# One visit of TensorE to attention for each chunk from the fifth tile on, in a fused state-space and MoE kernel

## The chip, the cores and the metric

The kernel runs on one core of a Trainium2 chip. The metric is the device time of one execution in microseconds. Five engines work side by side: TensorE (PE, with its weight loads shown apart as PEld), VectorE (DVE), ScalarE (ACT), GpSimd (POOL) and SyncE (SP), which here issues the DMAs.

## The reference

A chunked linear recurrence (called attention here) gives x of 3072 tokens and 256 features; an MLP follows, with g = h - tanh(h).

```python
log_a = np.log(np.clip(a, 1e-06, 1.0))            # batch 4, 8 heads, 768 steps
for c in range(nc):
    cum = np.cumsum(la, axis=-1)
    L = np.exp(cum[:, :, :, None] - cum[:, :, None, :]) * causal
    CB = np.einsum('bhin,bhjn->bhij', Cc, Bc)       # n = 16
    y_intra = np.einsum('bhij,bhjd->bhid', CB * L, xc)   # d = 32
    y_inter = np.einsum('bhin,bhnd->bhid', Cc, state) * np.exp(cum)[..., None]
    y[:, :, sl] = y_intra + y_inter
    state = decay_full[:, :, None, None] * state + np.sum(Bx, axis=2)
x = attn_out.transpose(0, 2, 1, 3).reshape(B * S, H * D)
h = x @ w_in                                        # 256 -> 2048
g = h - np.tanh(h)
return g @ w_out                                    # 2048 -> 256
```

## The kernel before

**The MLP.** The 3072 tokens form 12 tiles of 256; the 2048 hidden features form 8 units of 256. For each tile and unit there is one call of `mm1` (x by w_in into the PSUM tile ph) and one of `mm2` (g by w_out into the PSUM tile o). Every operand is split into a high part and a remainder (xh and xl, wh and wl, gh and gl), and three of the four products are kept, so a call is 12 matmuls of 128x256. A call is a **block** below; there are 192. Between the two, ACT takes the tanh (L542), DVE subtracts (L546), ACT makes gh (L550) and DVE gl (L557). There are two buffers of ph. The first four tiles are swept two units at a time (`SWEEPS`), since the weights arrive and are converted (`conv`, L280 to L304) meanwhile; from the fifth tile on each tile runs through its eight units.

**Attention.** The reference's chunks of 32 are taken in chunks of 112 steps, seven for each batch (the last has 96), 28 in all. The first 16 rows of a chunk's matrix carry the state of the chunk before. A chunk takes two pieces of work on TensorE:

- the **scores piece**, in `chunk_a`: four bf16 matmuls give the differences of the cumulated logs (L435) and eight small ones C B^T (L441), into the PSUM tile att. Behind it come the exponential on ACT (L445), the product on DVE (L449) and the causal select on POOL (L452), which makes lt. There is one buffer of att.
- the **y piece**, in `chunk_y`: eight matmuls give y (L477), and eight with a stationary operand of 16 columns give the next state (L485; left out for a batch's last chunk). It needs lt. Behind it ACT copies the state to the next chunk's x (L490) and makes xh (L497), and DVE makes xl (L502).

Where TensorE leaves the blocks for one or more such pieces and comes back, the text says a **visit**.

**The order** is made at build time. The code above calls `op(engine, cost, fn, r=..., w=...)`; nothing is issued then. `Order.issue` plays a list schedule of all operations with these costs 16 times, with priorities from a backward pass plus a random jitter of a fixed seed, keeps the shortest and issues each engine's instructions in that order. An `op` is never split, so the instructions of one `fn` stay together on their engine. Since priorities and jitter go by an operation's number, another set of operations gives another order everywhere. The main loop at the end lays out the calls of `mm1`, `mm2`, `chunk_a` and `chunk_y`.

```python
op("PE", 0.65, fn_p, r=[d["n_bc"], l_c[s], r_c[s]], w=[n_a])        # L456, scores
op("PE", 0.5 if last else 0.7, fn, r=[*k["n_l"], d["p_x"][cg], d["n_bw"]], w=[n_y])  # L505, y and state
```

Of the kernel before, what the change touches and what calls it, by code (L numbers as in the profile page):

```python
# [29 lines left out]
NCK = NB * CPB  # L30
# [13 lines left out]
NPH, NL, NSW, NRAW, NGB, LAG, WARM = 2, 3, 4, 2, 3, 2, 8  # L44
# [3 lines left out]
class Order:  # L48
# [12 lines left out]
    def slot(self, tag, bufs):  # L61
        k = self.count[tag] = self.count.get(tag, -1) + 1
        self.fresh[f"{tag}#{k}"] = tag, f"{tag}#{k - bufs}"
        return f"{tag}#{k}"
# [126 lines left out]
def tile_ssm_moe(ctx: ExitStack, tc: tile.TileContext, a, x, bn, bc, wts, out):  # L191
# [11 lines left out]
    op = Order()  # L203
    slot = op.slot
    grp = {g: {} for g in range(NG)}
    chs = {c: {} for c in range(NCK)}
    raws, gs, po, n_po, obs, misc = {}, {}, {}, {}, {}, {}

    chunks, ends = {}, 0
# [4 lines left out]
    wv, wm, pts, n_pt = {}, {}, {}, {}  # L214
    seq = {b: {} for b in range(NB)}
    KB = P * 1024

    SPAN = slice(len(chunks[0]), len(chunks[0]) + 7), slice(len(chunks[0]) + 7, NCK)


    def load_bc(G):
# [5 lines left out]
        def fn(i):  # L227
            if i == 0:
                d["bc"] = p2.tile([P, 2, CPG * (P + Q)], F32, tag="bc", name=f"bc{G}", bufs=NGB)
            nc.sync.dma_start(out=d["bc"][32 * i : 32 * i + N], in_=bc[G, i])  # L230

        for i in range(4):
            op("SP", 0.42, lambda i=i: fn(i), w=[d["n_bc"]], dma=KB // 2)
    def load_x(G):

        d = grp[G]
        d["n_x"] = slot("x", NGB)
        d["p_x"] = op.pieces(d["n_x"], CPG)

        def fn():  # L240
            d["x"] = p2.tile([P, CPG, H * D], F32, tag="x", name=f"x{G}", bufs=NGB)
            nc.sync.dma_start(out=d["x"], in_=x[:, G * CPG : (G + 1) * CPG])

        op("SP", 0.42, fn, w=d["p_x"], dma=2 * KB)

    def load_b(G):
# [5 lines left out]

        op("SP", 0.42, fn, w=[d["n_b"]], dma=KB)

    def load_w(u):
        name = raws[u, 0] = op.pieces(slot("raw", NRAW), 2)

        def fn(i):
            if i == 0:
                raws[u] = p2.tile([P, 2, 512, 2], U32, tag="raw", name=f"raw{u}", bufs=NRAW)  # L260
            nc.sync.dma_start(out=raws[u][:, i].rearrange("p k two -> p (k two)"), in_=wts[:, u, i])

        for i in range(2):
            op("SP", 0.42, lambda i=i: fn(i), w=[name[i]], dma=4 * KB)

# [74 lines left out]
    def qlen(ck):  # L340
        return QL if ck % CPB == CPB - 1 else Q
# [13 lines left out]
    def first_tile():  # L355
# [39 lines left out]
        for ck in range(len(chunks[0])):  # L395
# [12 lines left out]
            if ck in (0, 2):  # L408
# [7 lines left out]
                for i in range(4):  # L416
                    for j in range(2):
                        op("SP", 0.42, lambda i=i, j=j, sl=sl: get_parts(i, j, sl), r=["cum3"], w=[(l_c, r_c)[j][s]],
                           dma=(KB // 2, KB)[s])
            chunk_y(ck)  # L420

    def chunk_a(ck):

        d, k, q = grp[ck // CPG], chs[ck], qlen(ck)
        n_l = k["n_l"] = [slot("lt", NL)]
        n_a = k["n_a"] = slot("att", 1)

        def fn_p():  # L430
            at_ = ps_a.tile([P, 4, 4 * P], F32, tag="att", name=f"att{ck}")
            at_ = k["a"] = at_[:, :, 0 : 4 * q].rearrange("p i (k q) -> p i k q", k=4)
            for i in range(4):
                r = slice(32 * i, 32 * i + 9)
                nc.tensor.matmul(out=at_[:, i, 0:2, :], lhsT=lt_c[r, ck], rhs=rt_c[r, :, ck, N : N + q],  # L435
                                 start=True, stop=True)
            bb, cc = operands(ck)
            for w in range(2):
                for i in range(4):
                    r = slice(32 * i, 32 * i + N)  # L440
                    nc.tensor.matmul(out=at_[:, i, 2 + w, :], lhsT=bb[r, w], rhs=cc[r, w, 0:q], start=True, stop=True)  # L441

        def fn_e():
            k["l"] = p3.tile([P, H, Q], F32, tag="lt", name=f"lt{ck}", bufs=NL)
            nc.scalar.activation(k["l"][:, :, 0:q].rearrange("p (i w) q -> p i w q", i=4), k["a"][:, :, 0:2, :], AF.Exp)  # L445

        def fn_m():
            lt = k["l"][:, :, 0:q].rearrange("p (i w) q -> p i w q", i=4)
            nc.vector.tensor_tensor(out=lt, in0=k["a"][:, :, 2:4, :], in1=lt, op=ALU.mult)  # L449

        def fn_s():
            nc.gpsimd.affine_select(out=k["l"][:, :, 0:q], in_=k["l"][:, :, 0:q], pattern=[[0, H], [1, q]],  # L452
                                    compare_op=ALU.is_ge, fill=0.0, base=N, channel_multiplier=-1)

        s = ck >= SPAN[0].stop
        op("PE", 0.65, fn_p, r=[d["n_bc"], l_c[s], r_c[s]], w=[n_a])  # L456
        op("ACT", 0.92, fn_e, r=[n_a], w=n_l)
        op("DVE", 1.08, fn_m, r=[n_a], w=n_l)
        op("POOL", 1.4, fn_s, w=n_l)

    def chunk_y(ck):

        d, k, q = grp[ck // CPG], chs[ck], qlen(ck)
        b, c = divmod(ck, CPB)
        cg = ck % CPG
        n_y = slot("y", 1)
        last = c == CPB - 1
        if c == 0:
            seq[b]["n_xh"] = op.pieces(slot("xh", 2), CPB)
            seq[b]["n_xl"] = op.pieces(slot("xl", 2), CPB)  # L470
        n_xh, n_xl = seq[b]["n_xh"][c], seq[b]["n_xl"][c]

        def fn():
            y = k["y"] = ps_y.tile([P, 2 * H * D], F32, tag="y", name=f"y{ck}")
            for hg in range(2):
                for h in range(4):
                    nc.tensor.matmul(out=y[D * h : D * h + D, hg * Q : hg * Q + q],  # L477
                                     lhsT=d["x"][:, cg, P * hg + D * h : P * hg + D * h + D],
                                     rhs=k["l"][:, 4 * hg + h, 0:q], start=True, stop=True)
            if not last:  # L480

                for w in range(2):
                    for i in range(4):
                        h = 2 * i + w
                        nc.tensor.matmul(out=y[D * i : D * i + N, H * D + D * w : H * D + D * w + D],  # L485
                                         lhsT=d["b"][:, cg, N * h : N * h + N], rhs=d["x"][:, cg, D * h : D * h + D],
                                         start=True, stop=True)

        def fn_c(i):
            nc.scalar.copy(grp[(ck + 1) // CPG]["x"][0:N, (ck + 1) % CPG, 2 * D * i : 2 * D * i + 2 * D],  # L490
                           k["y"][D * i : D * i + N, H * D : H * D + 2 * D])

        def fn_h():
            if c == 0:
                seq[b]["xh"] = p3.tile([P, 2, S], F32R, tag="xh", name=f"xh{b}", bufs=2)
            k["yv"] = k["y"][:, 0 : 2 * Q].rearrange("p (g q) -> p g q", g=2)[:, :, 0:q]
            nc.scalar.copy(seq[b]["xh"][:, :, c * Q : c * Q + q], k["yv"])  # L497

        def fn_l():
            if c == 0:  # L500
                seq[b]["xl"] = p3.tile([P, 2, S], F32R, tag="xl", name=f"xl{b}", bufs=2)
            nc.vector.tensor_tensor(out=seq[b]["xl"][:, :, c * Q : c * Q + q], in0=k["yv"],  # L502
                                    in1=seq[b]["xh"][:, :, c * Q : c * Q + q].bitcast(F32), op=ALU.subtract)

        op("PE", 0.5 if last else 0.7, fn, r=[*k["n_l"], d["p_x"][cg], d["n_bw"]], w=[n_y])  # L505
        if not last:
            for i in range(4):
                op("ACT", 0.2, lambda i=i: fn_c(i), r=[n_y], w=[grp[(ck + 1) // CPG]["p_x"][(ck + 1) % CPG]])
        op("ACT", 0.36, fn_h, r=[n_y], w=[n_xh])
        op("DVE", 0.4, fn_l, r=[n_y, n_xh], w=[n_xl])  # L510
# [92 lines left out]
    def store(t, seg):  # L603
# [20 lines left out]
        for i in range(2):  # L624
            op("SP", 0.42, lambda i=i: fn_d(i), r=[name[i]], dma=KB)

# [17 lines left out]
    rest = p2.tile([P, 2, TT], F32, tag="ob", name="rest")[:, 0].rearrange("p (i q) -> p i q", i=2)  # L644
# [64 lines left out]
    l_c = op.pieces("lt_c", 2)  # L709
    r_c = op.pieces("rt_c", 2)  # L710
# [39 lines left out]
    def get_parts(i, k, sl):  # L750
        src = cum3[i // 2].rearrange("p (e w c) m -> p e w c m", e=2, w=2)[:, i % 2, :, sl].rearrange("p w c m -> p w (c m)")
        if k == 0:
            nc.sync.dma_start(out=lt_c[32 * i + 3 : 32 * i + 9, sl], in_=src)
        else:
            nc.sync.dma_start(out=rt_c[32 * i : 32 * i + 3, :, sl].rearrange("p w c m -> p w (c m)"), in_=src)
# [12 lines left out]
       r=[n_pq2], w=["wdec"])  # L768
# [19 lines left out]
    def plan(g, fn, *args):  # L788
        todo.setdefault(max(g, 0), []).append((fn, args))
# [5 lines left out]
    at_ = {}  # L795
# [2 lines left out]
        for i, ck in enumerate(chunks[t]):  # L798
            at_[ck] = g0 + i * n // len(chunks[t]), min(g0 + i * n // len(chunks[t]) + 1, g0 + n - 1)
    for ck in at_:  # L800
        plan(at_[ck][0], chunk_a, ck)
        plan(at_[ck][1], chunk_y, ck)
        if (ck + 1) % CPG == 0 and ck // CPG + NGB < NG:
            plan(at_[ck][1], group, ck // CPG + NGB)
# [58 lines left out]
```

## Time and profile before

| | us |
|---|---|
| time, median of 3 runs | 346.46 (345.67 to 348.44) |
| the profiled execution's own time | 350.21 |
| span of its trace, first to last instruction | 348.5 |
| PE busy | 333.0 (96%) |
| DVE busy | 228.1 (65%) |
| ACT busy | 193.0 (55%) |
| POOL busy | 53.8 (15%) |

The busy share of an engine is a mean over the whole span; which engine sets the time in a stretch has to be read from that stretch. The profiled execution is one of its own, and lies above the three timed ones.

### The profile page before, as it was taken

The page shows a single profiled execution, that of the slowest core. Times are in us where ns is not written, and L with a number is a line of the kernel's source. Part 1 is how long each engine was busy: PE and PEld are TensorE (multiplying, and loading weights), DVE is VectorE, ACT ScalarE, POOL GpSimd, SP SyncE. Part 2 cuts the span into 40 slices and gives each one's busy share as a digit, 9 for nine tenths or more (in the row PEclk, how much of TensorE's full clock was granted, in tenths as well). Part 3 has the DMA queues.
Part 4 walks back from the last instruction along what each step waited for, and adds up shares of the span by engine and source line. Part 5 has one row for each costly group of instructions (what it writes and reads, how often), then busy time and mean ns, then how long its engine had stood idle before and what let it go on. Part 6 is the DMA issues. An engine that isn't in the chain of part 4 may idle for free.

```text
span 348.5 us, 8864 instructions
## 1 busy us (share of the span) xinstructions
PE 333.0 (96%) x3756; PEld 320.0 (92%) x3756; DVE 228.1 (65%) x339; ACT 193.0 (55%) x403; POOL 53.8 (15%) x69
## 2 busy tenths in 40 slices
PE   9768779999999999999999999999999999999995
PEld 7657678899999999999999999999999999999995
DVE  5799976998998856545645654655645554655552
ACT  8767656986554443544555545544655545543441
POOL 1543343220000100020121210210211110110000
PEclk9868668999999999999999999999999999999999
DMA  6948583570100001111110300300300100000000
GB/s 186 259 115 286 137 282 78 158 184 5 40 3 0 2 32 37 57 30 45 57 46 8 85 2 2 88 2 2 90 3 1 32 2 2 32 0 2 30 2 31
DMA packets 12471, 21.39 MB, mean 61 GB/s; under 512 B 2848, under 2 KB 7648, under 8 KB 12432
## 3 DMA queue, kind: packets, MB, share of 16 engines
q1 hardware_dynamic: 12432, 20.84, 20.7%
q8 instruction: 29, 0.48, 0.6%
q14 instruction: 10, 0.08, 0.1%
HBM read 17.51 MB, written 3.32 MB: 60 GB/s over the span
## 4 chain that ended last, share of the span: by engine, by line
PE 84%; DVE 7%; ACT 2%; issue 2%; DMA 2%; SPq 1%; POOL 0%; DVEq 0%; POOLq 0%; ACTq 0%
PE o L578 38%; PE ph L528 37%; PE y L477 3%; PE att L441 3%; DMA bc<-bc_d 2%; DVE lt L449 1%; PE att L435 1%; DVE wl L304 1%; DVE gl L557 1%; SPq L230 1%; PE y L485 1%; DVE xl L502 1%; DVE wm L293 1%; DVE wm L285 1%; ACT lt L445 1%
## 5 line engine op out<-in xcount | busy, mean ns | idle before, releaser
L542 ACT ACTIVATE g<-ph 128x512 f32<-128x512 f32 x96 | 57.4, 598 | 96.6 <-PE ph L528 95.1
L546 DVE TENSOR_TENSOR g<-ph,g 128x512 f32<-128x512 f32 x96 | 66.1, 690 | 68.2 <-ACT g L542 68.1
L528 PE MATMUL ph<-xh,wh 128*128 128x256 f32 x384 | 101.5, 286 | 0.0
L528 PE MATMUL ph<-xh,wl 128*128 128x256 f32 x384 | 100.1, 283 | 0.4 <-DVE wl L304 0.4
L557 DVE TENSOR_TENSOR gl<-g,gh 128x512 fp32r<-128x512 f32 x96 | 67.3, 701 | 25.8 <-ACT gh L550 24.0
L528 PE MATMUL ph<-xl,wh 128*128 128x256 f32 x384 | 77.1, 282 | 0.0
L528 PEld LDWEIGHTS ph<-xh,wh 128*128 128x128 f32 x384 | 74.0, 193 | 1.0 <-issue 0.4
L528 PEld LDWEIGHTS ph<-xh,wl 128*128 128x128 f32 x384 | 73.8, 192 | 0.7 <-DVE wl L304 0.7
L550 ACT CAST gh<-g 128x512 fp32r<-128x512 f32 x96 | 59.1, 617 | 26.8 <-DVE g L546 25.2
L578 PE MATMUL o<-gh,wh 128*128 128x256 f32 x384 | 64.2, 289 | 0.1
L452 POOL TENSOR_SCALAR_AFFINE_SELECT lt<-lt 128x896 f32<-128x896 f32 (+1 forms) x25 | 30.9, 1236 | 215.6 <-DVE lt L449 214.6
L578 PE MATMUL o<-gl,wh 128*128 128x256 f32 x384 | 60.6, 280 | 0.0
L578 PE MATMUL o<-gh,wl 128*128 128x256 f32 x384 | 60.5, 279 | 0.0
L528 PEld LDWEIGHTS ph<-xl,wh 128*128 128x128 f32 x384 | 59.7, 192 | 0.0
L578 PEld LDWEIGHTS o<-gh,wh 128*128 128x128 f32 x384 | 51.6, 189 | 3.2 <-ACT pt L599 0.3
L578 PEld LDWEIGHTS o<-gl,wh 128*128 128x128 f32 x384 | 51.9, 189 | 0.0
L578 PEld LDWEIGHTS o<-gh,wl 128*128 128x128 f32 x384 | 51.9, 189 | 0.0
L449 DVE TENSOR_TENSOR lt<-att,lt 128x896 f32<-128x896 f32 (+1 forms) x25 | 26.7, 1067 | 5.8 <-ACT lt L445 5.8
L445 ACT ACTIVATE lt<-att 128x896 f32<-128x896 f32 (+1 forms) x25 | 22.5, 901 | 4.9 <-PE att L441 3.5
L490 ACT COPY x<-y 16x64 f32<-16x64 f32 x96 | 19.5, 203 | 7.0 <-DVE xl L502 6.0
L477 PE MATMUL y<-lt,x 128*32 128x112 f32 (+1 forms) x448 | 17.9, 282 | 3.6 <-POOL lt L392 3.3
L477 PEld LDWEIGHTS y<-lt,x 128*32 128x32 f32 x448 | 10.6, 116 | 7.6 <-POOL lt L392 3.6
(70 smaller groups left out, 232.7 us busy)
## 6 DMA issues: line engine op xcount, KB each, us to landing
raw<-w_d SPq DMA_DIRECT2D x16, 512.0 KB
x<-x_d SPq DMA_DIRECT2D x14, 256.0 KB
bc<-bc_d SPq DMA_DIRECT2D x56, 60.0 KB
out_d<-ob SPq DMA_DIRECT2D x24, 128.0 KB
braw<-bn_d SPq DMA_DIRECT2D x14, 112.0 KB
cum<-parts SPq DMA_DIRECT2D x1, 168.0 KB
lt_c<-cum SPq DMA_DIRECT2D x4, 27.0 KB
rt_c<-cum SPq DMA_DIRECT2D x4, 27.0 KB
```

Of the source, the lines that this page charges most:

```text
L441: nc.tensor.matmul(out=at_[:, i, 2 + w, :], lhsT=bb[r, w], rhs=cc[r, w, 0:q], start=True, stop=True)
L445: nc.scalar.activation(k["l"][:, :, 0:q].rearrange("p (i w) q -> p i w q", i=4), k["a"][:, :, 0:2, :], AF.Exp)
L449: nc.vector.tensor_tensor(out=lt, in0=k["a"][:, :, 2:4, :], in1=lt, op=ALU.mult)
L452: nc.gpsimd.affine_select(out=k["l"][:, :, 0:q], in_=k["l"][:, :, 0:q], pattern=[[0, H], [1, q]], compare_op=ALU.is_ge, fill=0.0, base=N, ...
L477: nc.tensor.matmul(out=y[D * h : D * h + D, hg * Q : hg * Q + q], lhsT=d["x"][:, cg, P * hg + D * h : P * hg + D * h + D], rhs=k["l"][:, 4 ...
L490: nc.scalar.copy(grp[(ck + 1) // CPG]["x"][0:N, (ck + 1) % CPG, 2 * D * i : 2 * D * i + 2 * D], k["y"][D * i : D * i + N, H * D : H * D + ...
L528: nc.tensor.matmul(out=ph[:, j, :], lhsT=w_[:, u, 0, k, j * P : (j + 1) * P], rhs=d[("xh", "xl")[p]][:, k, ts], start=p == 0 and k == 0 an ...
L542: nc.scalar.activation(g, gs[t, u][0], AF.Tanh)
L546: nc.vector.tensor_tensor(out=g, in0=ph, in1=g, op=ALU.subtract)
L550: nc.scalar.copy(gh, gs[t, u][1])
L557: on.tensor_tensor(out=gl, in0=g, in1=gh.bitcast(F32), op=ALU.subtract)
L578: nc.tensor.matmul(out=po[t, seg][:, e, :], lhsT=w_[:, u, 1, j, e * P : (e + 1) * P], rhs=g[:, j, :], start=u == seg[0] and k == 0 and j = ...
```

## The change

`chunk_a` no longer registers its operations itself from the fifth tile's first chunk on (`JOINT`, chunk 10). It hands its PE function on, and `chunk_y` of the chunk before registers one PE operation that issues y, the state, and then the next chunk's scores; the operations that follow the scores are registered right after it (`chunk_b`). Up to chunk 9 the scores are an operation of their own, as before. The last chunk's y has no scores behind it. No instruction is added or removed on any engine.

```diff
+    JOINT = chunks[NSW][0]
...
         s = ck >= SPAN[0].stop
-        op("PE", 0.65, fn_p, r=[d["n_bc"], l_c[s], r_c[s]], w=[n_a])
+        k["rest"] = fn_e, fn_m, fn_s
+        k["pe_a"] = fn_p, [d["n_bc"], l_c[s], r_c[s]], [n_a]
+        if ck < JOINT:
+            op("PE", 0.65, fn_p, r=k["pe_a"][1], w=k["pe_a"][2])
+            chunk_b(ck)
+
+    def chunk_b(ck):
+        k = chs[ck]
+        n_l, n_a = k["n_l"], k["n_a"]
+        fn_e, fn_m, fn_s = k["rest"]
         op("ACT", 0.92, fn_e, r=[n_a], w=n_l)
         op("DVE", 1.08, fn_m, r=[n_a], w=n_l)
         op("POOL", 1.4, fn_s, w=n_l)
...
-        op("PE", 0.5 if last else 0.7, fn, r=[*k["n_l"], d["p_x"][cg], d["n_bw"]], w=[n_y])
+        r, w, cost = [*k["n_l"], d["p_x"][cg], d["n_bw"]], [n_y], 0.5 if last else 0.7
+        if JOINT <= ck + 1 < NCK:
+
+            chunk_a(ck + 1)
+            fn_p, r_a, w_a = chs[ck + 1]["pe_a"]
+            op("PE", cost + 0.45, lambda: (fn(), fn_p()), r=r + r_a, w=w + w_a)
+            chunk_b(ck + 1)
+        else:
+            op("PE", cost, fn, r=r, w=w)
...
     for ck in at_:
-        plan(at_[ck][0], chunk_a, ck)
+        if ck < JOINT:
+            plan(at_[ck][0], chunk_a, ck)
         plan(at_[ck][1], chunk_y, ck)
```

TensorE in the fourth batch, before: y and state of chunk 23 and, one `mm2` block later, the scores of chunk 24 (y, att, o: the PSUM tiles; bc: B and C; bw: weighted B; the numbers behind a name count tiles).

```order
L477 MATMUL y_3719<-lt_3665,x_2796 32x112 x8
L485 MATMUL y_3719<-x_2796,bw_2793 16x32 x8
L578 MATMUL o_0_3511<-gh_5_3668,wh 128x256 x4
L578 MATMUL o_0_3511<-gh_5_3668,wl 128x256 x4
L578 MATMUL o_0_3511<-gl_5_3684,wh 128x256 x4
L435 LDWEIGHTS lt_c
L435 MATMUL att_3758<-rt_c,lt_c 128x224
...
L441 MATMUL att_3758<-bc_3069 128x112 x8
L578 MATMUL o_0_3511<-gh_6_3715,wh 128x256 x4
```

TensorE at the same two pieces in the changed kernel (lines moved by 2 to 19).

```order
L488 MATMUL y_3687<-lt_3582,x_2775 32x112 x8
L496 MATMUL y_3687<-x_2775,bw_2777 16x32 x8
L437 LDWEIGHTS lt_c
L437 MATMUL att_3704<-rt_c,lt_c 128x224
...
L443 MATMUL att_3704<-bc_2888 128x112 x8
L597 MATMUL o_0_3569<-gh_4_3651,wh 128x256 x4
```

The block between the two pieces is gone from there; the visit now begins with y and ends with the scores. From y of chunk 9 on, 34 visits have become 19: before, three of the 34 held both pieces, now 18 of the 19 do. Between those 19 the changed order has 18, 30, 6, 4, 12, 4, 7, 5, 4, 12, 4, 12, 4, 7, 5, 4, 12 and 4 blocks, and 10 blocks stand ahead of y of chunk 9, where it was 11.

ScalarE at the same place, before: around the exponential of chunk 24.

```order
L497 CAST xh_3524<-y_3719 128x2x112
L490 COPY x_3165<-y_3719 16x64 x3
L550 CAST gh_7_3756<-g_7_3736 128x512
L490 COPY x_3165<-y_3719 16x64
L445 ACTIVATE lt_3786<-att_3758 128x896
```

ScalarE there in the changed kernel.

```order
L561 ACTIVATE g_6_3717<-ph_6_3670 128x512
L508 CAST xh_3471<-y_3687 128x2x112
L447 ACTIVATE lt_3733<-att_3704 128x896
L569 CAST gh_6_3749<-g_6_3717 128x512
L501 COPY x_3127<-y_3687 16x64 x4
```

The exponential has moved ahead of the state's four copies and of a cast; one cast of y stands between it and the visit.

VectorE in the start-up, before: up to the xl of chunk 9 (y_934), with which the fourth tile's x is complete.

```order
L285 TENSOR_SCALAR wm_845<-raw_702 128x1024
L290 TENSOR_SCALAR wv_837<-wv_837 128x1024
L449 TENSOR_TENSOR lt_843<-att_807,lt_843 128x896
L502 TENSOR_TENSOR xl_804<-y_849,xh_796 128x2x112
L557 TENSOR_TENSOR gl_0_906<-g_0_821,gh_0_879 128x512
L546 TENSOR_TENSOR g_1_891<-ph_1_824,g_1_891 128x512
L293 SCALAR_TENSOR_TENSOR wm_845<-wv_837,wm_845 128x1024
L557 TENSOR_TENSOR gl_1_952<-g_1_891,gh_1_928 128x512
L449 TENSOR_TENSOR lt_911<-att_893,lt_911 128x896
L502 TENSOR_TENSOR xl_804<-y_934,xh_796 128x2x112
```

VectorE there in the changed kernel (chunk 9 is y_884), and what follows it.

```order
L513 TENSOR_TENSOR xl_802<-y_824,xh_779 128x2x112
L299 SCALAR_TENSOR_TENSOR wv_631<-wv_631,wm_655 128x1024
L576 TENSOR_TENSOR gl_0_916<-g_0_804,gh_0_878 128x512
L565 TENSOR_TENSOR g_1_882<-ph_1_845,g_1_882 128x512
L287 TENSOR_SCALAR wm_939<-raw_699 128x1024
L513 TENSOR_TENSOR xl_802<-y_884,xh_779 128x2x112
L292 TENSOR_SCALAR wv_842<-wv_842 128x1024
L576 TENSOR_TENSOR gl_1_964<-g_1_882,gh_1_942 128x512
L306 TENSOR_TENSOR wl<-wv_631,wh 128x1024
L295 SCALAR_TENSOR_TENSOR wm_939<-wv_842,wm_939 128x1024
```

Counted from the kernel's start, one L290, one L293, one L557 and one L449 that stood ahead of this xl now stand behind it; all else ahead of it is the same in kind and number.

## Rows read from the trace of the kernel before

**Rows 1.** Windows: busy us and instructions of each engine, granted TensorE clock, DMA.

```profile
core 0: us, PE busy (x) PEld busy (x) DVE busy (x) ACT busy (x) POOL busy (x), PEclk, DMA share, GB/s
23.40:69.00 45.60, 40.52 (x561) 36.59 (x556) 40.30 (x50) 31.60 (x69) 16.45 (x17) 0.80 0.66 192
50.00:55.00 5.00, 5.00 (x53) 4.67 (x50) 2.88 (x4) 1.76 (x5) 3.35 (x4) 0.50 0.23 41
69.00:314.50 245.50, 245.25 (x2717) 238.54 (x2716) 155.85 (x227) 130.62 (x265) 28.10 (x31) 1.00 0.11 32
86.00:141.50 55.50, 55.50 (x492) 55.50 (x491) 43.17 (x63) 27.32 (x49) 1.77 (x2) 1.00 0.07 22
```

**Rows 2.** Chain of waits, 300 to 312 us: start, length, what; two visits.

```profile
300.40 1.41 PE ph L528 x12
301.81 0.52 PE y L477 x16
...
302.44 1.56 PE o L578 x12
304.00 1.36 PE ph L528 x12
...
308.08 0.19 PE att L435 x4
...
308.73 1.61 PE o L578 x12
310.34 1.41 PE ph L528 x12
```

**Rows 3.** Chain of waits, 248 to 253 us: a visit with both pieces.

```profile
248.88 0.52 PE y L477 x16
...
250.17 1.61 PE o L578 x12
251.78 1.41 PE ph L528 x12
```

**Rows 4.** Chain of waits, 137 to 147 us: a visit of y and state.

```profile
137.66 2.72 PE ph L528 x24
...
142.38 1.61 PE o L578 x12
143.99 2.83 PE ph L528 x24
```

**Rows 5.** Timeline of all engines, 250 to 256 us, behind the visit of rows 3.

```profile
250.03 0.34 ACT L497 CAST xh<-y 128x224 fp32r<-128x224 f32 x1
250.10 0.74 PE L578 MATMUL o<-gh,wh 128*128 128x256 f32 x4
250.31 0.92 ACT L445 ACTIVATE lt<-att 128x896 f32<-128x896 f32 x1
251.26 1.09 DVE L449 TENSOR_TENSOR lt<-att,lt 128x896 f32<-128x896 f32 x1 [0.46 <-ACT lt L445]
252.42 1.37 POOL L452 TENSOR_SCALAR_AFFINE_SELECT lt<-lt 128x896 f32<-128x896 f32 x1 [2.13 <-DVE lt L449]
255.95 0.59 PE L477 MATMUL y<-lt,x 128*32 128x112 f32 x16
```

**Rows 6.** Groups of instructions, shapes apart: busy us and mean ns, idle before.

```profile
L557 DVE TENSOR_TENSOR gl<-g,gh 128x512 fp32r<-128x512 f32 x96 | 67.3, 701 | 25.8 <-ACT gh L550 24.0
L449 DVE TENSOR_TENSOR lt<-att,lt 128x896 f32<-128x896 f32 x21 | 22.8, 1088 | 5.2 <-ACT lt L445 5.2
L293 DVE SCALAR_TENSOR_TENSOR wm<-wv,wm 128x1024 uint32<-128x1024 uint32 x7 | 9.1, 1301 | 0.1
L290 DVE TENSOR_SCALAR wv<-wv 128x1024 f32<-128x1024 f32 x7 | 5.2, 741 | 0.0
```

**Rows 7.** Chain of waits, 50 to 57 us: two blocks of the start-up.

```profile
50.05 2.86 PE o L578 x12
...
54.02 2.25 PE ph L528 x12
```

## The prediction

> **What bounds the kernel now.** I read the windows first, to cut the span into stretches by who waits. From 23.4 to 69 us DVE is busy 40.30 of 45.60 us and PE 40.52, at a mean granted clock of 0.80: weights are converted, the first ten chunks run, and no engine alone sets the time [rows 1]. From 69 to 314.5 us PE is busy 245.25 of 245.50 us at clock 1.00, DVE 155.85 and ACT 130.62 [rows 1]. So in 70% of the span the time is the sum of PE's own work: blocks and visits. The reader should see there that nothing can be gained or lost except in the length of a block, in what a visit costs, or in a wait that does not exist yet.
>
> Then I read the chain of waits for those lengths, and two things show.
>
> First, a visit costs more than its own matmuls. The visit of y and state starts at 301.81 and the next block at 302.44, 0.63 us; but that block takes 1.56 where the one behind it takes 1.36, so 0.20 goes on coming back: 0.83 in all. The scores alone: 308.08 to 308.73, 0.65, and 1.61 against 1.41, together 0.85 [rows 2]. A visit with both: 248.88 to 250.17, 1.29, and again 1.61 against 1.41, together 1.49 [rows 3].
>
> Second, a block has two lengths at the same granted clock of 1.00. It takes 1.41 us ahead of the state visit at 301.81 and 1.36 behind it; behind the scores visit at 308.08 it is 1.41 again [rows 2]. A length holds until the next visit: from 85.7 to 141.7 us, 41 blocks without a visit all run at 1.36 [rows 1, 4]. I sorted all visits from 69 us on by what they end with. Those that end with the scores (16 alone, 3 behind a y piece) are followed by the long block every time, 19 of 19. Those that end with the state's matmuls, whose stationary operand has 16 columns, are followed by the short block 9 times in 12, as at 302.44, and 3 times by the long one, as at 142.38 [rows 2, 4]. The three y pieces without a state do not shorten it. I do not know why; the prediction uses only that it is so.
>
> **The change part by part.**
>
> *Joining.* From y of chunk 9 on there are 34 visits now and 19 in the changed order, so 15 fewer. Each joining saves 0.83 + 0.85 - 1.49 = 0.19 us [rows 2, 3]: what PE pays to leave the blocks and come back, once in place of twice. 15 x 0.19 = 2.9 us saved, all of it on PE, which bounds.
>
> *What a visit ends with.* Every joined visit ends with the scores. So behind chunk 9 no visit is left that ends with the state's matmuls, and by the 19 of 19 every block from there on has the long form. Short blocks now: 41 from 85.7 us, then 1, 5, 4, 4, 1, 5, 4 and 4 behind the other eight visits, 69 in all. Two blocks take 2.72 in the one form and 2.83 in the other [rows 4], 0.055 each: 69 x 0.055 = 3.8 us lost. The bounds are zero, if the length is not tied to the last piece, and 3.8.
>
> *Waits.* The joined operation waits for the lt of its own chunk, and for the att buffer and bc of the next. Blocks queue behind it on PE if it waits. The att buffer is free whenever lt is there, since the product that reads att comes before the select. The exposed chain is scores, exponential, product, select, y. At the joined visit of 248.88 it runs: visit over at 250.10, exponential 250.31 for 0.92, product to 252.35, select 252.42 to 253.79: 3.69 us behind the visit [rows 5]. In the changed order the shortest gap between joined visits is four blocks, seven times; that is the gap of this very place, where y starts at 255.95 without a wait, 2.16 us after the select. The four state copies now stand behind the exponential on ACT, and only the cast of y, 0.34, between the visit and it, as here [rows 5]. A further 0.3 to 0.6 us of queueing fits. I take zero. The copies come later than before but need not end until the next visit, over five microseconds on. The DMA queue issues the same transfers; its share is 0.11 in this stretch [rows 1].
>
> *The start-up.* The joining begins at chunk 10, but the planner's order is new everywhere, from the first chunk. I cost it where tile four becomes ready, at the xl of chunk 9, since behind it PE has blocks enough. Ahead of that xl DVE does one L290, one L293, one L557 and one L449 less: 0.74 + 1.30 + 0.70 + 1.09 = 3.8 us [rows 6]. The L557 belongs to a block that PE also has not done by then (10 blocks for 11), which it does later for 1.4. So at best 2.4 us are gained. DVE is at 40.30 of 45.60 there, not at all of it, and the chunk's own chain shares the bound, so I take half, 1.2. On the other side, this stretch holds pieces at half clock: at 50 to 55 us the clock is 0.50 [rows 1], and a block takes 2.86 instead of 1.41 [rows 7]. Where such a stretch falls depends on PE's pauses, which the new order moves. Two more such blocks would cost 2 x 1.45 = 2.9. So between 2.4 gained and 2.9 lost; 1.2 gained is nearer to the rows that can be counted.
>
> *Behind 314.5 us* there is no visit, and blocks have the long form already: zero.
>
> *Sum.* -2.9 + 3.8 + 0 - 1.2 = -0.3 us. Against the profiled execution's own time that gives 350.2 - 0.3 = 349.9; that execution lies 3.7 above the median of the runs, so for the median I set the same difference: 346.5 - 0.3 = 346.2.
>
> **The rivals.**
>
> *One length of block (faster).* If the block's length has nothing to do with the last piece, the saving of the joins stays: 346.5 - 2.9 - 1.2 = 342.4. For it speaks that 3 of 12 state visits give the long block, so something else has a say; against it the 19 of 19, three of them with exactly the joined order. The Trainium skill has a rule of this kind, in "TensorE: Matmul & The Clock Gate", Part 1, "Wait — 56ns, not 53.3ns?": at full clock matmuls follow each other after the moving columns divided by 2.4 GHz plus about 2.5 ns, whatever ran before. By that rule 256 columns would be an estimated 109 ns and a block 1.31 us, always. The trace differs, with 1.36 / 12 = 113 ns and 1.41 / 12 = 118 ns at clock 1.00 [rows 2], so I give this rival little.
>
> *The chain does not fit the four-block gaps (slower).* Place: y of the joined visit waits for the select. It decides once the chain grows by more than the 2.16 us that are free, for instance if the exponential and the product each come behind another piece of their own length (0.92 + 1.09) and a cast more (0.34). Grown by 3.2 us it would hold PE for 1.0 in each of seven gaps, 7.0 us, and the pace is lost as well: 346.5 - 2.9 + 3.8 - 1.2 + 7.0 = 353.2. Against it: the same gap holds at 248.88 with room, and ACT and DVE are busy little over half of the time.
>
> *Half clock in the start-up (slower).* If the new order opens one more pause ahead of two blocks: -2.9 + 3.8 + 2.9 = +3.8, 350.3. It decides from two more such blocks on. For it: the mean clock of 0.80 there shows how often it happens now [rows 1]; against it: fewer DVE instructions ahead of the chunks mean shorter pauses.
>
> That the change does not do what it says is out: the order shows 18 joined visits.
>
> **How the numbers follow.** A measurement of this kernel can tell about 1%, 3.5 us, from no change. Forecast 0.62 at 346.2, with its own range from 344.3 (start-up gains 2.4, a little pace kept) to 348.5 (no gain in the start-up and runs that lie as high as the highest now). One length of block 0.13 at 342.4; chain 0.07 at 353.2; half clock 0.13 at 350.3; 0.05 for a start-up that gains more than I can count. Range 342.2 to 350.5: it takes in the first rival and the third and leaves the chain and the far ends. Faster by over 1%, below 343.0: 0.11 of the first rival and 0.07 of the rest, 0.18. Slower, above 349.9: the chain, 0.09 of the half clock and 0.04 from the forecast's tail, 0.20. Within: 0.62.
>
> **What would show it.** In the changed profile's chain, joined visits of 1.29 us with 1.61 behind them, and behind each of them blocks of 1.41 and none of 1.36, above all from 85 to 142 us: that is the second term. Any idle time of PE ahead of L488 behind 70 us is the second rival. The first block of the stretch without idle time, against 69 us now, and the count of half-clock blocks before it give the start-up. I am wrong if short blocks survive, if PE waits for the select, or if the start-up moves by more than 3 us.

## The result, and the profile of the changed kernel

The changed kernel takes 344.38 us (median of 6 runs, 343.87 to 345.23), the kernel before in the same session 347.94 (median of 6, 345.67 to 348.44; the first three of them are those shown above). The ratio is 0.991, 95% interval 0.9882 to 0.9939: 3.1 us faster, between 2.1 and 4.1. That is inside the range, 1.8 us below the predicted 346.2, and 2.8 more gain than the sum of -0.3. By the medians alone the gain is 3.6; the time misses by less than the gain, since the kernel before came out 1.4 us above the 346.5 that the prediction started from. The profiled execution took 344.03 with a span of 342.3 us. That of before took 350.21, 2.3 above the median of its six runs; so the distance between the two profiles, 6.2, is twice the distance between the kernels, and half of it must be a matter of the one execution.

The page of the changed kernel: busy time of each engine, and the granted clock in 40 slices.

```profile
PE 328.4 (96%) x3756; PEld 317.9 (93%) x3756; DVE 227.5 (66%) x339; ACT 192.8 (56%) x403; POOL 52.1 (15%) x69
...
PEclk9956999999999999999999999999999999999999
```

PE is busy 4.6 us less than the 333.0 before. Next the windows of the changed kernel, which answer to [rows 1].

```profile
23.40:69.00 45.60, 41.80 (x591) 39.08 (x586) 43.38 (x56) 35.03 (x74) 16.58 (x18) 0.92 0.78 223
50.00:55.00 5.00, 5.00 (x99) 4.63 (x101) 4.75 (x7) 4.10 (x11) 2.50 (x4) 1.00 0.65 122
65.00:300.00 235.00, 235.00 (x2648) 229.61 (x2647) 150.19 (x218) 125.53 (x256) 27.48 (x32) 1.00 0.11 32
```

PE has no idle time left from 65 us on: 235.00 of 235.00. From 23.4 to 69 us its granted clock is 0.92 where it was 0.80, and from 50 to 55 us, where before ran at 0.50, it does 99 matmuls for 53. This one execution gains in the start-up.

The chain of waits of the changed kernel: first the long stretch of [rows 4], then a joined visit and the four blocks behind it.

```profile
85.63 2.83 PE ph L547 x24
...
265.81 0.52 PE y L488 x16
266.33 0.12 PE y L496 x16
266.44 0.21 PE att L437 x4
266.65 0.45 PE att L443 x16
267.10 1.61 PE ph L547 x12
268.71 1.41 PE o L597 x12
270.13 2.83 PE ph L547 x24
272.95 0.52 PE y L488 x16
```

The joined visit takes 1.29 us (265.81 to 267.10) and the block behind it 1.61, as in [rows 3]. From 57 us to the end no block of 1.36 is found; the stretch of 85 us runs at 2.83 for two blocks where [rows 4] shows 2.72.

The timeline behind that visit, as [rows 5].

```profile
267.24 0.92 ACT L447 ACTIVATE lt<-att 128x896 f32<-128x896 f32 x1 [0.77 <-PE att L443]
...
268.19 1.09 DVE L451 TENSOR_TENSOR lt<-att,lt 128x896 f32<-128x896 f32 x1 [1.00 <-ACT lt L447]
...
269.35 0.99 POOL L454 TENSOR_SCALAR_AFFINE_SELECT lt<-lt 128x896 f32<-128x896 f32 x1 [7.19 <-DVE lt L451]
```

The exponential now comes right behind the visit, and lt is there at 270.34, 2.6 us before the next y at 272.95. The four-block gap holds with as much room as before.

The DVE instructions of [rows 6] cost nearly the same (713 ns for 701, 1089 for 1088): they are only at other places.

```profile
L576 DVE TENSOR_TENSOR gl<-g,gh 128x512 fp32r<-128x512 f32 x96 | 68.4, 713 | 28.7 <-ACT gh L569 27.4
L451 DVE TENSOR_TENSOR lt<-att,lt 128x896 f32<-128x896 f32 x21 | 22.9, 1089 | 8.4 <-ACT lt L447 8.2
```

So in this trace the joins save what they should, the pace is lost as foreseen, no wait came, and the start-up gained far more than 1.2 us. The experiments ask which of this belongs to the kernels and which to one execution, and whether the pace has the reason that the prediction gave.

### The profile page after: what moved, and what is told of

Its sections match the earlier page's. It is cut to its first block, busy times and chain, and to the rows that moved or that the text cites. A ratio compares the mean times of both kernels' runs of the same rounds, so it can differ in the third digit from the quotient of the medians.

```text
span 342.3 us, 8855 instructions
## 1 busy us (share of the span) xinstructions
PE 328.4 (96%) x3756; PEld 317.9 (93%) x3756; DVE 227.5 (66%) x339; ACT 192.8 (56%) x403; POOL 52.1 (15%) x69
## 4 chain that ended last, share of the span: by engine, by line
PE 88%; DMA 3%; DVE 3%; SPq 2%; ACT 1%; issue 1%; POOL 1%; POOLq 0%
PE ph L547 40%; PE o L597 40%; PE y L488 4%; PE att L443 3%; DMA raw<-w_d 2%; DMA bc<-bc_d 1%; PE att L437 1%; SPq L232 1%; PE y L496 1%; DVE lt L451 1%; DVE wm L295 0%; DVE gl L576 0%; DVE wv L299 0%; POOL bw L330 0%; ACT x L501 0%
## 5 line engine op out<-in xcount | busy, mean ns | idle before, releaser
L576 DVE TENSOR_TENSOR gl<-g,gh 128x512 fp32r<-128x512 f32 x96 | 68.4, 713 | 28.7 <-ACT gh L569 27.4
L569 ACT CAST gh<-g 128x512 fp32r<-128x512 f32 x96 | 59.3, 619 | 34.1 <-DVE g L565 32.9
L547 PEld LDWEIGHTS ph<-xh,wh 128*128 128x128 f32 x384 | 73.2, 191 | 1.4 <-issue 0.4
L597 PE MATMUL o<-gh,wh 128*128 128x256 f32 x384 | 62.3, 284 | 0.0
L454 POOL TENSOR_SCALAR_AFFINE_SELECT lt<-lt 128x896 f32<-128x896 f32 (+1 forms) x25 | 28.3, 1131 | 155.4 <-DVE lt L451 152.8
L488 PE MATMUL y<-lt,x 128*32 128x112 f32 (+1 forms) x448 | 17.1, 272 | 6.5 <-POOL bc L337 2.5
L330 POOL TENSOR_TENSOR bw<-braw,wdec 128x256 f32<-128x256 f32 x14 | 12.5, 896 | 52.8 <-PE y L496 47.1
```

Source lines behind the costliest of these rows:

```text
L330: nc.gpsimd.tensor_tensor(out=d["b"].rearrange("p c (h n) -> p c h n", h=H), in0=d["braw"].rearrange("p c (h n) -> p c h n", h=H), in1=wd. ...
L547: nc.tensor.matmul(out=ph[:, j, :], lhsT=w_[:, u, 0, k, j * P : (j + 1) * P], rhs=d[("xh", "xl")[p]][:, k, ts], start=p == 0 and k == 0 an ...
L569: nc.scalar.copy(gh, gs[t, u][1])
L576: on.tensor_tensor(out=gl, in0=g, in1=gh.bitcast(F32), op=ALU.subtract)
L597: nc.tensor.matmul(out=po[t, seg][:, e, :], lhsT=w_[:, u, 1, j, e * P : (e + 1) * P], rhs=g[:, j, :], start=u == seg[0] and k == 0 and j = ...
```

## The experiments

Each ratio is to runs of the kernel before on the same chip in the same session, whose median was 347.9 to 348.4 us.

**e1_flip: the joined visit ends with the state.** If the last piece sets the length of the blocks, this keeps the joins and brings the short blocks.

```diff
-            op("PE", cost + 0.45, lambda: (fn(), fn_p()), r=r + r_a, w=w + w_a)
+            op("PE", cost + 0.45, lambda: (fn_p(), fn()), r=r + r_a, w=w + w_a)
```

> The changed kernel with the two pieces of a joined visit in the other order: scores first, then y and state; all else as in the changed kernel. Theory (what a visit ends with sets the length of the blocks behind it): the 130 blocks behind a visit that now ends with the state's matmuls become short, 0.055 us each, for all or for 9 in 12 of the visits: 5.4 to 7.1 us less than the changed kernel's 344.4, so 337.3 to 339.0; the chain of waits shows blocks of 1.36. Rival (the long block comes with any visit that holds scores, wherever they stand): 344.4, blocks of 1.41. Start-up as in the changed kernel in both.

Measured: 345.25 us, ratio 0.993 (0.9895 to 0.9966). The chain of waits of this kernel around one of its joined visits:

```profile
268.97 0.21 PE att L437 x4
269.18 0.45 PE att L443 x16
269.63 0.52 PE y L488 x16
270.15 0.12 PE y L496 x16
270.26 1.61 PE ph L547 x12
271.88 1.41 PE o L597 x12
```

The visit ends with the state's matmuls, and still every block behind it is long. That the last piece sets the length is refuted. From the end of the visit of chunk 9 to the end of the trace, e1 and the changed kernel both take 286.7 us: the order of the two pieces costs nothing.

**e2_again: the scores first issue, then a matmul of the state once more at the end.** The order of the change stays, and only the very last matmul of a joined visit is one with 16 columns (it writes the same values to the same place once more).

```diff
-            op("PE", cost + 0.45, lambda: (fn(), fn_p()), r=r + r_a, w=w + w_a)
+            op("PE", cost + 0.45, lambda: (fn(), fn_p(), fn_again()), r=r + r_a, w=w + w_a)
```

> The changed kernel with one more matmul at the end of each joined visit that has a state: the last of the eight 16-column state matmuls (32 moving columns) is done once more, with the same result. Theory (the kind of the very last matmul decides): short blocks behind 16 of 18 joined visits, up to 7.1 us less, against 16 times an extra matmul and a change of shape, 0.05 to 0.2 us each: 338 to 342. Rival (it takes the whole y and state piece, or the order of the pieces as such): 345 to 347, blocks of 1.41.

Measured: 347.71 us, ratio 1.0011 (0.998 to 1.0042), slightly above the rival's 345 to 347. The visits take 1.45 us instead of 1.29, the blocks stay long. It is 2.5 above e1 on the same chip, which the longer visits explain: 16 x 0.16 = 2.6. With e1 this settles that neither the last piece nor the last matmul decides.

**e3_join_only: the joins without the new order.** In the order of before, each scores piece from chunk 13 on is moved right behind y and state of the chunk ahead; all else, the start-up too, stays as it was. That makes 13 visits fewer.

```diff
+        for ck in range(13, NCK):
+            order.remove(self.i_a[ck])
+            order.insert(order.index(self.i_y[ck - 1]) + 1, self.i_a[ck])
```

> The kernel before, its order kept instruction for instruction, but from chunk 13 on the scores are moved to stand right behind y and state of the chunk before. The start-up is that of before, so this is the joining alone. Theory: 13 visits fewer at 0.19 us, 2.5 us saved, and the 28 short blocks behind 142 us become long, 1.5 us lost; 0.9 us less than before: 347.0 where before has 347.9, and a trace that is the same as before's up to 142 us. Then the rest of the change's gain came from the start-up. Rival (joining itself is worth more, and the start-up little): 344 to 345.

Measured: 347.14 us, ratio 0.9966 (0.9937 to 0.9996), 1.2 us faster. The chain of waits of this kernel:

```profile
253.01 0.52 PE y L485 x16
253.53 0.12 PE y L493 x16
253.65 0.21 PE att L443 x4
253.86 0.45 PE att L449 x16
254.31 1.61 PE o L586 x12
255.92 1.41 PE ph L536 x12
```

Joined visits of 1.30 with long blocks again. But here also the 41 blocks from 81 us on were long, at 118 ns from matmul to matmul, though nothing ahead of them was changed. That pointed to the profile of before itself.

**e4_join_flip: the same with the scores ahead of y and state.**

```diff
-            order.insert(order.index(self.i_y[ck - 1]) + 1, self.i_a[ck])
+            order.insert(order.index(self.i_y[ck - 1]) + 0, self.i_a[ck])
```

> As the run before it, but the scores are moved to stand right ahead of y and state, so that the joined visits end with the state. Theory: 2.5 us saved by 13 visits fewer, and of the 106 blocks between chunk 12 and chunk 27 the 90 behind a state become short, all or 9 in 12, where 28 are short now: 2.2 to 3.4 us saved; 342.0 to 343.2 where before has 347.9. Rival (order of the pieces does not matter): as the run before it.

Measured: 347.58 us, ratio 0.9981 (0.9956 to 1.0006). A miss for the theory of the last piece: no short block stands behind any of these visits, and the time is that of e3 within their intervals.

**e5_before_2nd and e6_before_3rd: the kernel before, profiled twice more.** No edit.

> The kernel before, unchanged, profiled a second time, to see what belongs to the kernel and what to one execution. If short blocks (1.36) are fixed by the instructions, they stand behind the same nine state visits as in the first profile, 69 blocks in all. If they come by chance behind a visit that holds y and state alone, there are some, behind other visits, between 0 and 69 blocks. The start-up: 11 blocks and chunk 9 were done at 63.7 us in the first profile; the same order in the two runs with moved scores had them at 59.3 and 58.7, so 58.5 to 64 here.

> The kernel before, unchanged, profiled a third time; the same two theories on the short blocks, and 58.5 to 64 us for the start-up.

Measured: 348.99 and 348.26 us (one run each). The chain of waits of e6, at the long stretch and behind a lone visit of y and state:

```profile
81.61 3.02 PE o L578 x24
84.63 2.83 PE ph L528 x24
...
300.45 1.56 PE o L578 x12
302.01 1.36 PE ph L528 x12
```

The 41 blocks that [rows 4] shows at 2.72 for two run at 2.83 in both. The other short blocks of the first profile are here again, in both, behind the same eight visits: 1, 5, 4, 4, 1, 5, 4 and 4, together 28. So of the 69 short blocks that the prediction counted, 28 belong to the kernel and 41 to the one execution that it was read from.

**e7_after_2nd: the changed kernel, profiled once more.** No edit.

> The changed kernel, unchanged, profiled a second time. No short block behind any of the 18 joined visits by either theory. The start-up: 10 blocks, chunk 9 and the scores of chunk 10 were done at 55.6 us in the first profile, 58.8 and 59.1 in the two runs that share its start-up order; if that scatter belongs to the execution, 55 to 59.5 here, and 57 to 61 with the block that the kernel before has done by then: 1 to 2 us ahead of before in the mean, not the 6.7 of the two first profiles.

Measured: 346.74 us (one run). No short block behind any joined visit, as in the first profile. The visit of chunk 9 is over at 58.32 us, where the first profile has 55.6: the start-up of one kernel moves by 2.7 us from execution to execution.

**e8_split: the scores one block ahead of y and state.** A new theory came from sorting the visits of all these profiles by what stood ahead: short blocks stand behind a visit of y and state alone, if the visit before it held scores alone. In the order of the change the scores from chunk 13 on are put one block ahead of the visit they were joined to, which gives 15 visits more.

```diff
+        for i, (fn_p, ck) in self.joint.items():
+            p = [k for k, _ in todo].index(i)
+            p -= ck > 11
+            while ck > 11 and self.ops[todo[p][0]][0] != "PE":
+                p -= 1
...
+            todo.insert(p, (-i, fn_p))
```

> The changed kernel's order, kept instruction for instruction, but from chunk 13 on the scores stand one block ahead of y and state: 15 visits more. Theory (a visit costs 0.19 us of its own; short blocks come by chance behind visits with y and state alone): 2.9 us more than the changed kernel, less what short blocks give back, at most 64 of them at 0.055, 3.5 us: between 0.6 less and 2.9 more than the changed kernel's 344.4, joined by a trace with lone visits of 0.64 and 0.65 us. Rival (the joining gains nothing, the new order does): 344.4 with visits that sum to no more than joined ones.

Measured: 344.44 us (4 runs), ratio 0.9888 (0.9836 to 0.994). The chain of waits of this kernel:

```profile
265.55 0.21 PE att L447 x4
265.75 0.45 PE att L453 x16
266.20 1.60 PE o L609 x12
267.81 0.52 PE y L498 x16
268.33 0.12 PE y L506 x16
268.44 1.56 PE ph L559 x12
270.01 1.36 PE o L609 x12
```

Behind all 13 lone visits of y and state the blocks are short, 64 in all. They give 64 x 0.055 = 3.5 us and the 15 visits cost 15 x 0.19 = 2.9: the same time as the changed kernel by another road. The rival expects this time too; what speaks against it is the trace, with lone visits of 0.64 and 0.65 us and their longer first blocks.

**e9_behind: the scores one block behind y and state.** The opposite order at the same price in visits; little is left between the scores and the next scores' visit for the short form.

```diff
+            if ck > 11:
+                p += 1
+                while self.ops[todo[p][0]][0] != "PE":
+                    p += 1
+                todo.insert(p + 1, (-i, fn_p))
+                continue
```

> The changed kernel's order, but from chunk 13 on the scores stand one block behind y and state: as many visits as in the split run, of the same two kinds, with the long gaps behind the scores in place of behind the state. Theory (a visit costs 0.19 us of its own; blocks are short behind a visit of y and state alone whose predecessor was a visit of scores alone, until the next visit): 15 visits x 0.19 = 2.9 us lost, 13 blocks short, 0.7 back: 2.1 more than the changed kernel's 344.4, 346.5. Rival (separate visits are as good as joined ones in any order): 344.4, as the split run.

Measured: 349.78 us, ratio 1.0063 (1.0031 to 1.0095): 3.3 us slower than the 346.5 foreseen. The one block between y and the scores is short in 10 of the 12 places where the visit ahead held scores alone; the two others stand behind a stall of the kind that follows, as two of the ten do. The chain of waits of this kernel in a gap of four blocks:

```profile
271.97 0.21 PE att L453 x4
272.17 0.50 PE att L459 x16
...
272.76 0.93 ACT lt L463
...
273.71 1.09 DVE lt L467
...
275.04 0.69 DVE g L583
...
275.87 1.65 PE ph L565 x12
277.52 0.52 PE y L504 x16
```

The three blocks between the scores and the next y take 4.85 us here (272.67 to 277.52) instead of 1.61 + 1.41 + 1.41 = 4.43. The chain shows why: behind the scores come the exponential (0.93) and the product (1.09), and only then, with one xl (0.39) between, the subtraction L583 (0.69), which has to free a buffer of ph before the next `mm1` block goes on. Seven such gaps cost 7 x 0.42 = 2.9. With 2.9 for the visits and 10 x 0.055 = 0.6 for the short blocks that is +5.2 against the changed kernel; the medians differ by 5.4.

**e10_best: short blocks wherever the theory gives them.** As e8, but from chunk 11 on, so that the long stretch at 82 us is short as well; a batch's last chunk issues the state's matmuls too (nothing reads them), since y without them had long blocks behind it in e8; and the last scores stand one block behind y, so that the end runs short.

```diff
+            if ck == NCK - 2:
...
+                todo.insert(p + 1, (-i, fn_p))
+                continue
+            p -= ck >= 10
+            while ck >= 10 and self.ops[todo[p][0]][0] != "PE":
+                p -= 1
...
-            if not last:
+            if not last or JOINT <= ck:
```

> The split run carried on: scores one block ahead of y and state already from chunk 11 on; the last scores one block behind the state, three blocks ahead of the last y; and the 16 state matmuls also for a batch's last chunk, where nothing reads them. Theory: 145 short blocks in place of the split run's 64, 81 x 0.055 = 4.5 us less; two visits more, 0.4, and three times 0.12 us of state matmuls, 0.4: 3.7 less than the split run's 344.4, 340.7, with blocks of 1.36 behind every lone state visit, 28 of them at the end. Rival (short blocks have another cause): 344 to 346.

Measured: 340.72 us (6 runs, 340.17 to 341.62), ratio 0.9782 (0.9758 to 0.9806). The chain of waits of this kernel, at the long stretch, at y and state behind y and state, and at the end:

```profile
83.32 2.92 PE o L615 x24
86.24 2.72 PE ph L565 x24
...
289.65 1.61 PE ph L565 x12
...
297.27 2.92 PE o L615 x24
300.19 1.36 PE ph L565 x12
```

Behind 17 of 17 visits of y and state whose predecessor held scores alone the blocks are short, 145 in all, the 28 of the end among them; behind the one at 289.01, whose predecessor was again y and state, the block is long. This version is faster than the kernel before by 7.3 us in the same session (348.02) and than the changed one's 344.38 by 3.7.

**e11_before_seed and e12_after_seed: both kernels with another seed of the order's jitter.** The order changes everywhere, the change stays the same.

```diff
-    ROUNDS, JITTER, SEED = 16, 0.3, 133908
+    ROUNDS, JITTER, SEED = 16, 0.3, 1
```

> The kernel before with another seed of the planner's jitter: another order in the start-up, the same order of blocks and visits from 140 us on. If the start-up's part of the gain is a draw of the planner, its time moves by up to 2 us either way, 346 to 350. If only the joined operation frees the start-up, 348 as before. Chunk 9 is done behind 13 blocks here, not 11, so the point to compare is that visit less two blocks.

> The changed kernel with the same other seed: joined visits throughout, another start-up. Theory (joins 2.9 saved, 28 short blocks lost, 1.5; start-up a draw): 1.4 us less than before plus or minus 2: 344.5 to 348.5, and 0.5 to 2.5 less than before with that seed if their start-ups are alike. Rival (the change itself frees the start-up): 344.4 again.

Measured: 349.6 us, ratio 1.0047 (1.0019 to 1.0074), and 346.38 us, ratio 0.9942 (0.9922 to 0.9962). With this seed they are slower by 1.6 (0.0047 of 348.0) and by 2.0 (346.38 against 344.38), and the difference between the two is 3.2 us, as with the old one. So both draws of the order gain about as much. In e11 the same 28 blocks are short, and the 41 of the long stretch as well: with this seed a visit with scores alone (from 73.27 us) stands ahead of the y and state in front of them, which is the theory's condition. The chain of waits of e11 there:

```profile
84.08 0.52 PE y L477 x16
...
84.72 2.92 PE o L578 x24
```

In e12 all blocks behind 57 us are long. So this pair loses 3.8 us of pace where the other loses 1.5, and the timelines show where that is made up. The visit of chunk 9 is over at 61.41 us in e11 and at 57.36 in e12, each with 10 blocks done (not 13, as the expectation has it for e11): the start-up gains 4.0. From there to the end of the trace e11 takes 286.0 us and e12 287.2: joins and pace together lose 1.2. So far as these two profiles go, it is chance that both pairs gain alike, and 3.2 lies outside the 0.5 to 2.5 expected for start-ups that are alike, which these are not.

## Why the time lay in the range, and where the sum was wrong

The measured 344.38 lies at the edge of the 344.3 to 348.5 that the prediction gave its own forecast, and that it is inside is in part luck: two terms of the sum had the wrong size, and the kernel before came out slower than the start value.

**Joining, -2.9: right.** Every joined visit of y, state and scores behind 70 us takes 1.28 to 1.30 us and has a block of 1.61 behind it, in the changed kernel and in e1, e3 and e12. (The 34 visits of before include that of chunk 10's scores, one block ahead of y of chunk 9.) The step of the argument, what PE pays to leave the blocks and come back is paid once in place of twice, holds with its size of 0.19. The Trainium skill states in "TensorEngine Tiling (Array Packing)", Key Properties, that a change of the tiling mode drains TensorE. That fits the trace, where the first block behind a visit takes 0.20 longer than the next; that a drain is what costs the 0.20, no run here shows, and the page gives no price for it.

**"What a visit ends with", +3.8: the step that failed.** Its forecast of the rows came true, that no short block stands behind a joined visit. But its size was too large, and the reason was wrong. The size: the 69 short blocks were counted in one profile, and 41 of them were short in that execution alone. In the order of before the visit ahead of theirs holds both pieces; e3, e4, e5 and e6 leave that part as it is and show them long. What the change takes away as a rule is 28 x 0.055 = 1.5 us. The reason: e1, e2 and e4 end visits with the state and get long blocks. What fits instead is the pair of visits: short behind y and state alone, if the visit ahead held scores alone. Behind 69 us that was so 8 times of 8 in each of the three profiles of the kernel before, 9 of 9 in e11, 13 of 13 in e8 and 17 of 17 in e10, and 10 times of 12 in e9. Blocks were long behind joined visits in either order, and behind y and state whose predecessor was a joined visit or y and state, with one exception, and that is the 41 blocks of the first profile: the visit ahead of theirs, at 69.01 us, is a joined one. The sorting in the prediction had already shown 3 of 12 state visits with long blocks; it did not ask what stood ahead of them. Its other count is too high: from 69 us on 16 visits end with the scores (13 alone, 3 behind a y piece), not 19; all 16 have long blocks behind them.

**Waits, 0: right.** PE is busy 235.00 of 235.00 us, and the four-block gap has 2.6 us to spare. The rival of the chain that does not fit, 353.2, did not come. e9 shows that its place was well chosen all the same: with the scores one block later in the same gaps, PE loses 0.42 us in each. What it waits for then is not the select, though, but the subtraction that frees ph, queued behind the exponential and the product. The prediction passed over a wait that was there already: in before, the scores in the visit at 69 us wait for DVE's product (the visit takes 1.61 us, in e5 and e6 1.66 and 1.67, in place of 1.29), and the blocks behind it have a gap of 0.1. The changed kernel has neither, which gains up to 0.5.

**The start-up, -1.2: right in sign, somewhat small, and with a scatter that the range had to hold.** The chain of waits of the changed kernel at the visit of chunk 9:

```profile
54.38 0.52 PE y L488 x16
...
55.23 0.45 PE att L443 x16
55.67 1.61 PE o L597 x12
```

PE goes on here without a pause; it is over with chunk 9 at 55.7 (55.6 in the timeline). Taken from the timelines of all profiles that keep each order there, the time is 63.7, 60.3, 59.5, 59.3 and 58.7 for before (first profile, e5, e6, e3, e4), mean 60.3, with 11 blocks done; for the changed one 55.6, 58.8, 59.1, 58.3, 56.9, 55.6 and 56.1 (first, e1, e2, e7, e8, e9, e10), mean 57.2, with 10 blocks done, so 58.6 with the block added. The gain is 1.7 us in the mean of these few, and one execution differs from the next by up to 5.

The difference inside one order goes with the last stretch at half clock (granted clock 0.50, the lower level of 1.2 GHz): the slowest of before, its first profile, has it at 48.5 to 55.4 us, e5, e6 and e3 have one half as long between 47 and 52, and the fastest, e4, has none there; of the changed order the three slowest, e1, e2 and e7, are the three with such a stretch at 47 to 51 us. The first profile of the changed kernel has a single stretch, at 17.5 to 31.1 us, with 1.00 on both sides: PE was busy for 4.52 of the 7.5 us ahead of it, and for 6.58 of its last 7.1. With a late stretch the two orders are level (59.3 to 60.3 against 59.7 to 60.5 with the block added), without one the changed order is ahead (58.7, e4 alone, against 57.0 to 58.3). So the four DVE instructions fewer, the prediction's reason for its 1.2, are not shown to be the cause: no run separates them from where the half clock fell. By its own sign, a move of more than 3 us, the prediction would have been wrong on the two first profiles alone (63.7 against 57.0). The rival of more half clock, 350.3, did not come.

**The sum.** What lies behind the start-up can be read without its scatter: from the end of the visit of chunk 9 to the end of the trace, the same 181 blocks take 287.0 us in e5 and e6, 286.0 in e3, and 285.3 in the changed kernel (286.7 with a block more). e3 gives joins and pace alone: 13 x 0.19 = 2.5 saved, 1.5 lost, so -1.0, which is what these traces show; as times, -1.2 and, in e4, -0.7 were measured. The change gains 1.7 there: 14 joins save 2.7 (the 15th lies ahead of this point and is part of the start-up), the pace takes 1.5, the wait that is gone gives the rest. With the 1.7 of the start-up that makes 3.4; 3.1, between 2.1 and 4.1, was measured. The rival "one length of block", 342.4, had the right sign and a wrong reason: there are two lengths, and e10 earns its 3.7 us from the difference. By the rule that the prediction cites from the Trainium skill ("TensorE: Matmul & The Clock Gate", Part 1), an estimated 109 ns from matmul to matmul, neither would be seen; the runs show 113.3 and 117.8. The words "whatever ran before" are the prediction's: the page gives the rule for matmuls back to back, and here each has a weight load of its own.

## What to carry to other kernels

Before a term is built on a pattern in one profile, see whether it returns in a second profile of the same kernel: 41 of the 69 short blocks did not, and with them went 2.3 of the 3.8 us. Where an engine is busy without a gap, look at what its equal pieces of work cost one by one; here the length of a block, a difference of 4%, was worth more than the joins, and an order that makes more visits was the fastest. A gain that returns with another order need not have the same parts: in one pair of kernels the steady part gained 1.7, in the other it lost 1.2. And a work piece that is moved brings its followers on the other engines along: what then comes late can be a buffer that has nothing to do with it.

## What the runs showed of the hardware that was not expected

The same stream of 128x256 matmuls, with the granted clock at 1.00, runs at one of two steady paces, 113.3 or 117.8 ns from start to start, and keeps it for as long as no small matmuls come between (29 blocks in e10, 41 in the first profile of before). Weight loads take 188 ns at both. What sets the pace is known only as the rule above, with its exceptions: the 41 blocks, short in one execution of five, and the two places in e9; before 69 us both lengths occur behind like visits. Why the visit ahead of the last one matters, no run here shows, and it stays open.

The half-clock stretches of the start-up fall differently from execution to execution of one and the same order, and the end of the start-up shifts with them by up to 3.5 us in the changed order and 5 in that of before, more than most of the terms in this sum.
